# Attention, routing and two MoE layers on one core: the weight-narrowing steps and the first norm moved to other slots of an expert, low parts moved behind the gathers

## The chip, the cores and the metric

One NeuronCore of one Trainium2 chip runs the whole program; the other cores are idle. The metric is the device time of one execution in microseconds (us), as the median of several executions; lower is better. The engines are named as the profile names them: PE is TensorE (matrix products), PEld its weight loads, DVE VectorE, ACT ScalarE, POOL GpSimd, SP SyncE, which here only issues DMAs. A PE product has a granted clock, shown as a share of full speed (1.00 is 2.4 GHz, 0.50 is 1.2 GHz).

## The reference, cut to what matters

```python
for t in range(S):                                  # attention, 4 x 8 heads, 768 steps, head size 48
    state = f[:, :, t, :, None] * state + einsum('bhd,bhe->bhde', k[:, :, t], v[:, :, t])
    y[:, :, t] = einsum('bhd,bhde->bhe', q[:, :, t], state)
x = y, one row of 384 numbers for each of 3072 tokens
logits = x @ w_gate                                 # 8 experts, at most 384 tokens each, highest logits first
for e in range(8):                                  # first layer
    out[tokens of e] = maximum(x[tokens of e] @ w1[e], 0) @ w2[e]      # 384 -> 1024 -> 384
xn = out / sqrt(mean(out * out, axis=-1) + 1e-6) * rms_g               # norm
g = xn @ w_gate2;  val = xn @ w_val                 # second layer, 384 -> 1536
result = (g * sigmoid(g) * val) @ w_out             # 1536 -> 384
```

The three weight matrices of the second layer (`w_gate`, `w_val`, `w_out` of `moe2`) come as 64-bit floats.

## The kernel before, in words

**Stages.** Attention (0 to about 183 us of the span); routing, which finds by bisection which tokens each expert takes (to about 236 us); the eight experts of the first layer, one after the other (to about 464 us); the second layer in eight chunks of 384 tokens (to the end). All instructions of one engine run in the order in which the program issues them, since the schedule is written by hand (`manual_schedule`); between engines only semaphores order the work. PE gets its precision from three products for each fp32 product: an operand is split into a high part (`hi`, rounded to the format that PE multiplies in one pass, float32r) and a low part (`lo`, what is left), and `mm3` (lines 570 to 574) multiplies hi·hi, hi·lo and lo·hi. A high part is a copy on ACT, a low part a subtraction on DVE.

**An expert.** `expert(e)` (lines 1025 to 1045) has eight slots, j = 0 to 7. Slot j multiplies the expert's 384 tokens (`XT[e]`, hi and lo) with 128 columns of w1 (`h`, 9 products at lines 572 to 574), takes the high part with ReLU on ACT (`hh`, line 1036) and the low part on DVE (`hl`, line 1037), and from slot 2 on multiplies what slot j - 2 made with w2 (`second`, tile `x2`, 9 products). The last two `second` follow slot 7. So `hl` of slot j has two slots of PE work before it is due. Then `side(e, j)` (lines 992 to 1023) issues work beside PE:
- slot 0: the gathers of the next expert's token rows (`gather`, line 782, three indirect DMAs on POOL's queue) and a weight load on SP's queue;
- slots 1 to 4: one narrowing step, and one `piece_split` of the next expert's weights: hi by ACT (line 756), lo by DVE (line 759, 1536 numbers in each partition);
- slots 5 to 7: the transposition of one third of the next expert's tokens on PE (`xpose`, line 918, tile `xT`), its hi on ACT (line 928) and its lo on DVE (line 929); in slots 6 and 7 one narrowing step behind it.

**A narrowing step** (`narrow_step`, lines 972 to 978) turns a 36th of the 64-bit weights of the second layer into fp32 in a pipeline over several steps. One call issues, in this order: the write back to memory of a piece finished earlier (a DMA on ACT's queue, line 974), the arithmetic of a piece loaded two calls ago (`narrow2`: line 960 on ACT into `nr`; lines 961, 962 and 964 on DVE, the last into `ne`; lines 965 and 966 on POOL), and the load of another piece (a DMA on SP's queue, line 951). `ne` has one buffer, so line 964 of a step waits until line 965 of the step before has read it; `nb` has two, `nr` and `nraw` three. There are six calls in each of the experts 0 to 6, 42 in all, of which 40 do something.

**The first norm.** `Norm` (lines 853 to 890) of chunk 0 runs in the last expert's slots, by the table `NORM0`: the squares and their sum over the three blocks, with a hi and a lo part of the sum, in slot 0 (`squares`, lines 862 to 872); in slot 1 the sum over partitions, by two float32r products with a matrix of ones, and the square root (`total`, lines 874 to 878); the reciprocals in slots 2 to 4; the three scalings in slot 5; hi and lo of the scaled tokens (`prep`, line 897) in slot 6. The other chunks' norms run in the second layer.

**The seam between routing and expert 0.** `R.finish` ends with the token indices `idx` (line 303). Lines 829 to 832 then issue expert 0's three gathers on POOL, two subtractions for low parts of expert 0's weights on DVE (`low_part(0)` and `low_part(2)`, line 795), and the load of a flag into a register of every engine, on which each of them branches (line 833; the slow path behind it is not taken). Behind it come nine transpositions of the gathered rows (line 1051), the split of the tokens (`split`, lines 926 to 929), and the other two low parts (1 and 3, line 1055). Low part 0 and 1 belong to w1 of expert 0, 2 and 3 to its w2.

Of the kernel before, what the change touches and what calls it, by code (L numbers as in the profile page):

```python
# [7 lines left out]
F32 = mybir.dt.float32  # L8
F32R = mybir.dt.float32r
# [682 lines left out]
def tile_kernel(ctx, tc, q, k, v, f_logit, w_gate, w1, w2, w2_gate, w2_val, w2_out, rms_g, out):  # L692
# [107 lines left out]
    with ExitStack() as st:  # L800
        with tc.tile_pool(name="rw", bufs=6) as rw, tc.tile_pool(name="rwp", bufs=4, space=PSUM) as rwp:
            rows = Rows(tc, YT, x_dram, ident, rw, rwp)
            rows.put(1)
            rows.take(1)
            R = R[0]
            R.copy()
            w_load(0, 0)

            def side(s):
                if s < 0:  # L810
                    bank = rwp.tile([128, 4, 2, 64], F32, name="rows").rearrange("p a b c -> p (a b c)")
                    turn_inc(tc, K, bank[:, 0:128], ident)
                    return
                if s == 0:
                    more_consts(tc, rc, K)
                if s < 3:
                    w_load(0, s + 1)
                if 0 < s < 5:
                    pool, raw, shape, _ = W1[0, s - 1]
                    hi, lo = (pool.tile([128, 1536], F32R, name="w").rearrange("p (a b) -> p a b", a=shape[0])  # L820
                              for _ in range(2))
                    nc.scalar.copy(hi, raw)
                    parts[s - 1] = hi, lo, raw

            R.steps(6, rows, side)
            rows.put(2)
            rows.take(2)
            R.finish(flag, idx, ident, lambda: (rows.put(3), rows.take(3)))
            gather(0)
            for i in (0, 2):  # L830
                low_part(i)
        rv = nc.values_load(flag[0:1, 0:1], min_val=0, max_val=1)
        with tc.If(rv > 0):
            with tc.tile_pool(name="rb", bufs=1, space=PSUM) as rb:
                R.start(NT // 128, rb.tile([128, 256], F32, name="bank"))
            R.copy()
            R.steps(15)
            R.finish(flag, idx, ident)
            rv2 = nc.values_load(flag[0:1, 0:1], min_val=0, max_val=1)
            with tc.If(rv2 > 0):  # L840
                slow_attention(tc, q, k, v, f_logit, x_dram, w_gate, lg, lg_dram, ident)
                slow_route(tc, K, lg, A.rearrange("p e n -> p n e"), ident)
                slots(tc, K, A, ident, idx)
            gather(0)
# [6 lines left out]
    TC = CAP  # L851

    class Norm:


        def __init__(self, c, pool, psum, name, tmp=None, parts=None):
            self.parts = parts or (lambda: [pool.tile([128, TC], F32R, name=n) for n in ("sh", "sl")])
            self.x = xn[:, :, c * TC:(c + 1) * TC]
            self.pool, self.psum, self.name = pool, psum, name
            self.tmp = tmp or (lambda n: pool.tile([128, TC], F32, name=n))  # L860

        def squares(self):
# [4 lines left out]
                nc.scalar.activation(sq, self.x[:, m], AF.Square)  # L867
                nc.vector.tensor_tensor(out=s, in0=s, in1=sq, op=OP.add)
            self.s = s
            self.sh, self.sl = self.parts()  # L870
            nc.scalar.copy(self.sh, s)
            nc.vector.tensor_tensor(out=self.sl, in0=s, in1=self.sh.bitcast(F32), op=OP.subtract)

        def total(self):
            o = self.psum.tile([128, TC], F32, name=self.name)
            nc.tensor.matmul(o, ones, self.sh, start=True, stop=False)
            nc.tensor.matmul(o, ones, self.sl, start=False, stop=True)
            nc.scalar.activation(self.s, o, AF.Sqrt, bias=eps[:, 0:1], scale=1.0 / DM)

        def recip(self, i):  # L880
# [13 lines left out]
    def xt_tiles():  # L894
        return [xtp.tile([128, KD, CAP], F32R, name=n) for n in ("xhi", "xlo")]
# [7 lines left out]
    with ExitStack() as c1:  # L903
# [75 lines left out]

        X0 = []  # L980

        def first_parts():
            X0.extend(xt_tiles())
            return [t[:, 0] for t in X0]

        n0 = Norm(0, tp, psT, "xT", lambda n: nraw().rearrange("p c two -> p (c two)").bitcast(F32)[:, :TC], first_parts)
        NORM0 = {(E - 1, 0): n0.squares, (E - 1, 1): n0.total}
        tail0 = n0.steps()[2:]
        for i in range(2, 5):
            NORM0[E - 1, i] = tail0.pop(0)  # L990

        def side(e, j):
            if e + 1 < E:
                if j == 0:
                    gather(e + 1)
                    w_load(e + 1, 1)
                if 0 < j < 5:
                    narrow_step()
                    piece_split(W1[e + 1, j - 1])
                if j in (1, 2):  # L1000
                    w_load(e + 1, j + 1)
# [2 lines left out]
                if j == 7:  # L1004
                    if e + 2 < E:
                        w_load(e + 2, 0)
                    else:
                        w2_load(0)
                if j > 5:
                    narrow_step()  # L1010
            else:
                if j < 6:
                    w2_load(j + 1)
                if j:
                    piece_split(W2[j - 1])
                if j == 5:
                    for f in tail0:
                        f()
                if j == 6:
                    for d in range(KD):  # L1020
                        prep(0, d, X0, nc.gpsimd)
            if (e, j) in NORM0:
                NORM0[e, j]()

        def expert(e):
# [18 lines left out]
            second(e, KF - 1, x2, H)  # L1044
            finish(e, x2)

        XT[0] = xt_tiles()
        o = x2_tiles()
        for c in range(3):
# [1 line left out]
                nc.tensor.transpose(o[d][:, c * 128:(c + 1) * 128], XG[0][c][:, d * 128:(d + 1) * 128], ident)  # L1051
        for d in range(KD):
            split(0, d, o[d])
        for i in (1, 3):
            low_part(i)
        w_load(1, 0)
        for e in range(E):
# [116 lines left out]
```

## Time and profile before

| | |
|---|---|
| median of 3 executions | 926.68 us |
| lowest, highest | 925.27, 927.19 us |
| the profiled execution | 926.02 us |
| its span, first to last instruction | 924.3 us |
| mean granted clock of PE over the span | 0.968 |
| DVE busy over the span | 502.0 us (54%), 839 instructions |
| ACT busy over the span | 380.7 us (41%), 748 instructions |
| POOL busy over the span | 277.3 us (30%), 328 instructions |

All times of the trace are counted from the span's start. The profiled execution lies inside the spread of the three timed ones; 1.7 us of its time lie outside the span. Shares over the whole span say little about the experts: each stage has to be read by itself.

### The profile page before, as it was taken

The numbers are of one execution on the slowest core, as the hardware profiler recorded it, in microseconds if no ns is written. First come the engines' busy times: TensorE is split into PE (matmuls) and PEld (weight loads), VectorE is DVE, ScalarE is ACT, GpSimd is POOL, SyncE is SP. The second block draws the span as 40 slices with busy tenths as digits, with TensorE's granted clock in tenths as the row PEclk, the third lists the DMA queues.
The fourth block names the chain that finished last, engine by engine and source line by source line (L and its number), as shares of the span: only waits on it lengthen the run. The fifth ranks groups of instructions, "written<-read, shape, count | busy, mean of one in ns | idle before, by whom it ended". The sixth has DMA issues, their size and how long they took to land.

```text
span 924.3 us, 17642 instructions
## 1 busy us (share of the span) xinstructions
PE 876.3 (95%) x7263; PEld 844.5 (91%) x7263; DVE 502.0 (54%) x839; ACT 380.7 (41%) x748; POOL 277.3 (30%) x328
## 2 busy tenths in 40 slices
PE   7999999866699999999999999999999999999997
PEld 7889897755599999999899999999999999999996
DVE  6665666477679888886744333443324333343222
ACT  3444444366245555454752332423324232242221
POOL 3323333154557777773410201102011010100101
PEclk9999999965599999999999999999999999999999
DMA  9556551062567788776320000000000000000000
GB/s 207 122 114 135 110 119 28 1 219 109 190 243 246 248 296 290 266 243 218 104 69 1 26 1 1 27 1 26 1 1 26 1 27 2 1 26 1 26 1 26
DMA packets 70168, 87.73 MB, mean 95 GB/s; under 512 B 29632, under 2 KB 56256, under 8 KB 70080
## 3 DMA queue, kind: packets, MB, share of 16 engines
q1 hardware_dynamic: 61008, 70.00, 26.0%
q0 software_dynamic: 3072, 9.44, 3.1%
q10 hardware_dynamic: 6000, 7.09, 2.2%
q8 instruction: 58, 0.95, 0.4%
q14 instruction: 30, 0.25, 0.1%
HBM read 70.01 MB, written 16.52 MB: 94 GB/s over the span
## 4 chain that ended last, share of the span: by engine, by line
PE 71%; issue 11%; DVE 10%; POOL 3%; DMA 2%; ACT 1%; POOLq 0%; ACTq 0%; SPq 0%; DVEq 0%
PE bank L390 7%; PE yp L484 5%; PE v L574 4%; PE g L573 4%; PE v L573 4%; PE v L572 4%; PE g L574 4%; PE g L572 4%; PE o L573 4%; PE o L572 4%; PE o L574 4%; PE bank L450 3%; PE x L573 2%; PE x L574 2%; PE x L572 2%
## 5 line engine op out<-in xcount | busy, mean ns | idle before, releaser
L1112 DVE TENSOR_TENSOR hf<-sg,v 128x384 f32<-128x384 f32 x96 | 53.1, 553 | 193.8 <-PE v L574 164.6
L900 POOL TENSOR_TENSOR xlo<-xn,xhi 128x384 fp32r<-128x384 f32 x24 | 27.4, 1143 | 302.3 <-ACT xhi L899 302.3
L1115 ACT CAST hh<-hf 128x384 fp32r<-128x384 f32 x96 | 49.3, 513 | 139.0 <-DVE hf L1112 137.3
L573 PE MATMUL o<-w,hh 128*128 128x384 f32 x288 | 97.0, 337 | 0.0
L572 PE MATMUL o<-w,hh 128*128 128x384 f32 x288 | 96.6, 335 | 0.0
L573 PE MATMUL g<-xlo,w 128*128 128x384 f32 x288 | 96.6, 335 | 0.0
L574 PE MATMUL v<-xhi,w 128*128 128x384 f32 x288 | 96.6, 335 | 0.0
L572 PE MATMUL v<-xhi,w 128*128 128x384 f32 x288 | 96.6, 335 | 0.0
L573 PE MATMUL v<-xlo,w 128*128 128x384 f32 x288 | 96.5, 335 | 0.0
L574 PE MATMUL g<-xhi,w 128*128 128x384 f32 x288 | 96.5, 335 | 0.0
L574 PE MATMUL o<-w,hl 128*128 128x384 f32 x288 | 96.3, 334 | 0.0
L572 PE MATMUL g<-xhi,w 128*128 128x384 f32 x288 | 96.2, 334 | 0.0
L1110 ACT ACTIVATE sg<-g 128x384 f32<-128x384 f32 x96 | 47.1, 491 | 118.7 <-PE g L574 118.5
L1116 DVE TENSOR_TENSOR hl<-hf,hh 128x384 fp32r<-128x384 f32 x96 | 53.6, 559 | 55.6 <-ACT hh L1115 55.6
L965 POOL TENSOR_TENSOR nr<-nr,ne 128x384 f32<-128x384 f32 x36 | 62.4, 1734 | 46.5 <-DVE ne L964 17.3
L573 PE MATMUL x<-hl,w 128*128 128x384 f32 x192 | 65.7, 342 | 2.5 <-DVE hl L1037 2.2
L759 DVE TENSOR_TENSOR w<-wraw,w 128x1536 fp32r<-128x1536 f32 x35 | 64.6, 1845 | 5.3 <-ACT w L756 5.2
L572 PE MATMUL h<-xhi,w 128*128 128x384 f32 x192 | 67.1, 349 | 0.3 <-ACT xhi L928 0.3
L573 PE MATMUL h<-xlo,w 128*128 128x384 f32 x192 | 65.7, 342 | 0.0
L574 PE MATMUL h<-xhi,w 128*128 128x384 f32 x192 | 65.5, 341 | 0.0
L572 PE MATMUL x<-hh,w 128*128 128x384 f32 x192 | 65.3, 340 | 0.0
L457 POOL TENSOR_SCALAR_AFFINE_SELECT at<-at 128x384 f32<-128x384 f32 x62 | 31.5, 543 | 111.2 <-ACT at L456 111.1
(231 smaller groups left out, 2034.3 us busy)
## 6 DMA issues: line engine op xcount, KB each, us to landing
wraw<-in_moe_w_dram SPq DMA_DIRECT2D x32, 768.0 KB, 5.9
raw_f<-in_f_logit_dram SPq DMA_DIRECT2D x16, 288.0 KB, 3.4
raw_k<-in_k_dram SPq DMA_DIRECT2D x16, 288.0 KB, 5.0
raw_q<-in_q_dram SPq DMA_DIRECT2D x16, 288.0 KB, 5.0
v<-in_v_dram SPq DMA_DIRECT2D x32, 144.0 KB, 4.6
x_dram<-xrows SPq DMA_DIRECT2D x24, 192.0 KB, 1.9
nraw<-in_moe_w_gate_dram SPq DMA_DIRECT2D x12, 384.0 KB, 5.9
nraw<-in_moe_w_val_dram SPq DMA_DIRECT2D x12, 384.0 KB, 5.2
```

What stands on the lines that cost most here:

```text
L390: nc.tensor.matmul(o[64 * h:64 * h + 64, r * TP:(r + 1) * TP], t[:, c0:c0 + 64], ident[0:TP, 0:TP], start=True, stop=True)
L457: nc.gpsimd.affine_select(out=t, in_=t, pattern=[[0, 3], [1, C]], compare_op=OP.is_ge, fill=0.0, base=0, channel_multiplier=-1)
L484: nc.tensor.matmul(YP[n // 3][d, (n % 3) * C:(n % 3 + 1) * C], ST[i][d, :, n] if state else V[i % NV][:, n, h, :], QT[i][d, c] if state el ...
L572: nc.tensor.matmul(out, lhs[0], rhs[0], start=first, stop=False)
L573: nc.tensor.matmul(out, lhs[0], rhs[1], start=False, stop=False)
L574: nc.tensor.matmul(out, lhs[1], rhs[0], start=False, stop=last)
L759: eng.tensor_tensor(out=lo, in0=raw, in1=hi.bitcast(F32), op=OP.subtract)
L965: nc.gpsimd.tensor_tensor(out=r, in0=r, in1=e2.bitcast(F32), op=OP.mult)
L1110: nc.scalar.activation(sg, pg, AF.Silu)
L1112: nc.vector.tensor_tensor(out=h, in0=sg, in1=pv, op=OP.mult)
L1115: nc.scalar.copy(hh, h)
L1116: nc.vector.tensor_tensor(out=hl, in0=h, in1=hh.bitcast(F32), op=OP.subtract)
```

## The change

Three edits, all in what the hand-written order issues where.

1. The six narrowing steps of an expert stand in slots 0, 1, 4, 5, 6 and 7 instead of 1, 2, 3, 4, 6 and 7. In slot 0 the step stands behind the gathers and the weight load; in slots 5 to 7 behind the transposition.
2. The first norm's squares move from slot 0 of expert 7 to slot 7 of expert 6, behind everything else there, and its total from slot 1 to slot 0 of expert 7. For this chunk alone the sum isn't split: one fp32 product with ones takes the place of two float32r products, and a copy on ACT and a subtraction on DVE fall away. The reciprocals move to slots 1 to 3; scaling and `prep` of block 0, 1 and 2 stand in slots 4, 5 and 6, where `X0` is also allocated now.
3. `low_part(0)` moves behind the branch, ahead of expert 0's transpositions; `low_part(2)` moves behind the split, ahead of low parts 1 and 3.

```diff
@@ -827,8 +827,6 @@
             gather(0)
-            for i in (0, 2):
-                low_part(i)
         rv = nc.values_load(flag[0:1, 0:1], min_val=0, max_val=1)
...
@@ -867,14 +865,19 @@
             self.s = s
-            self.sh, self.sl = self.parts()
+            if not self.parts:
+                return
+            self.sh, self.sl = (self.pool.tile([128, TC], F32R, name=n) for n in ("sh", "sl"))
             nc.scalar.copy(self.sh, s)
...
         def total(self):
             o = self.psum.tile([128, TC], F32, name=self.name)
-            nc.tensor.matmul(o, ones, self.sh, start=True, stop=False)
-            nc.tensor.matmul(o, ones, self.sl, start=False, stop=True)
+            if self.parts:
+                nc.tensor.matmul(o, ones, self.sh, start=True, stop=False)
+                nc.tensor.matmul(o, ones, self.sl, start=False, stop=True)
+            else:
+                nc.tensor.matmul(o, onesf, self.s, start=True, stop=True)
...
-        NORM0 = {(E - 1, 0): n0.squares, (E - 1, 1): n0.total}
+        NORM0 = {(E - 2, 7): n0.squares, (E - 1, 0): n0.total}
         tail0 = n0.steps()[2:]
-        for i in range(2, 5):
+        for i in range(1, 4):
             NORM0[E - 1, i] = tail0.pop(0)
...
                     gather(e + 1)
                     w_load(e + 1, 1)
+                if j in (0, 1, 4):
+                    narrow_step()
                 if 0 < j < 5:
-                    narrow_step()
                     piece_split(W1[e + 1, j - 1])
...
-                if j > 5:
+                if j > 4:
                     narrow_step()
...
-                if j == 5:
-                    for f in tail0:
-                        f()
-                if j == 6:
-                    for d in range(KD):
-                        prep(0, d, X0, nc.gpsimd)
+                if j == 4:
+                    X0.extend(xt_tiles())
+                if 3 < j < 7:
+                    tail0[j - 4]()
+                    prep(0, j - 4, X0, nc.gpsimd)
...
+        low_part(0)
         XT[0] = xt_tiles()
...
         for d in range(KD):
             split(0, d, o[d])
-        for i in (1, 3):
+        for i in (2, 1, 3):
             low_part(i)
```

## Rows read from the trace of the kernel before

**Rows 1.** The page, section 1: busy us, share of the span, instructions

```profile
PE 876.3 (95%) x7263; PEld 844.5 (91%) x7263; DVE 502.0 (54%) x839; ACT 380.7 (41%) x748; POOL 277.3 (30%) x328
```

**Rows 2.** Waits of PE over the span: total us, times, longest us

```profile
PE x L1051 <- DMA xrow<-x_dram,idx: 6.7, 2, 6.0
...
PE x L573 <- DVE hl L1037: 2.2, 3, 0.8
```

**Rows 3.** Timeline of all engines at the seam: start us, us, what, [idle before]

```profile
236.38 3.43 DVE L795 TENSOR_TENSOR w<-wraw,w 128x1536 fp32r<-128x1536 f32 x2
236.47 2.75 POOL L782 DMA_INDIRECT xrow<-x_dram,idx  x1 [1.45 <-DVE idx L303]
239.52 1.11 POOL L782 DMA_INDIRECT xrow<-x_dram,idx  x1 [0.30 <-issue]
240.94 0.94 POOL L782 DMA_INDIRECT xrow<-x_dram,idx  x1 [0.30 <-remote]
...
245.23 0.69 PE L572 MATMUL h<-xhi,w 128*128 128x384 f32 x1 [0.28 <-ACT xhi L928]
...
246.61 3.42 DVE L795 TENSOR_TENSOR w<-wraw,w 128x1536 fp32r<-128x1536 f32 x2
...
249.95 0.55 DVE L1037 SCALAR_TENSOR_TENSOR hl<-h,hh 128x384 fp32r<-128x384 f32 x1
...
252.49 0.34 PE L573 MATMUL x<-hl,w 128*128 128x384 f32 x1
```

**Rows 4.** Line 833 (the branch) on DVE: ns min/median/max, first and last start

```profile
L833 DVEq EVENT_SEMAPHORE  x2: 21/21/21, 240.5 to 240.6; - x2
...
L833 DVEq COMPARE_BRANCH  x1: 72/72/72, 237.1 to 237.1; - x1
```

**Rows 5.** Table by stretch, all engines; PEclk is the granted clock

```profile
248.00:252.00 4.00, 4.00 (x20) 4.00 (x19) 3.03 (x4) 1.55 (x3) 0.00 (x0) 0.76 0.93 308
```

**Rows 6.** The same table: experts 1 to 6 together, expert 3, expert 4

```profile
273.79:436.63 162.84, 160.38 (x919) 157.02 (x919) 137.19 (x186) 87.26 (x141) 115.27 (x84) 1.00 0.79 264
328.00:355.62 27.62, 26.88 (x155) 26.20 (x154) 24.26 (x34) 14.87 (x25) 20.90 (x15) 1.00 0.80 265
355.62:382.37 26.75, 26.66 (x154) 26.23 (x154) 23.27 (x34) 14.78 (x25) 20.07 (x15) 1.00 0.81 269
```

**Rows 7.** Timeline of DVE in expert 3, slots 1 to 4

```profile
332.38 0.35 DVE L961 TENSOR_SCALAR nb<-nraw 128x384 int32<-128x384 int32 x1
...
333.77 1.76 DVE L759 TENSOR_TENSOR w<-wraw,w 128x1536 fp32r<-128x1536 f32 x1
...
340.96 0.55 DVE L1037 SCALAR_TENSOR_TENSOR hl<-h,hh 128x384 fp32r<-128x384 f32 x1
341.43 0.70 DVE L961 TENSOR_SCALAR nb<-nraw 128x384 int32<-128x384 int32 x1
...
343.80 1.75 DVE L759 TENSOR_TENSOR w<-wraw,w 128x1536 fp32r<-128x1536 f32 x1
```

**Rows 8.** Timeline of POOL in expert 3, slots 0 and 1

```profile
331.22 0.99 POOL L782 DMA_INDIRECT xrow<-x_dram,idx  x1
...
333.85 2.50 POOL L782 DMA_INDIRECT xrow<-x_dram,idx  x1 [0.30 <-issue]
336.37 1.03 POOL L965 TENSOR_TENSOR nr<-nr,ne 128x384 f32<-128x384 f32 x1
```

**Rows 9.** Timeline of PE at the first norm in expert 7

```profile
441.59 0.44 PE L876 MATMUL xT<-xhi,onesr 128*128 128x384 f32 x1 [1.61 <-ACT xhi L871]
442.18 0.44 PE L877 MATMUL xT<-xlo,onesr 128*128 128x384 f32 x1 [0.15 <-DVE xlo L872]
442.46 0.34 PE L572 MATMUL h<-xhi,w 128*128 128x384 f32 x1
442.64 0.34 PE L573 MATMUL h<-xlo,w 128*128 128x384 f32 x1
```

**Rows 10.** Groups of instructions, shapes apart: count, busy us, mean ns of one

```profile
L496 PE MATMUL bank<-YT,wgp 112*32 112x384 f32 x64 | 6.4, 492 | 0.0
```

More of the change, by code (lines that the diff above doesn't have):

```diff
@@ L853, in tile_kernel, with __init__ @@
     class Norm:
-        def __init__(self, c, pool, psum, name, tmp=None, parts=None):
-            self.parts = parts or (lambda: [pool.tile([128, TC], F32R, name=n) for n in ("sh", "sl")])
+        def __init__(self, c, pool, psum, name, tmp=None, parts=True):
+            self.parts = parts
             self.x = xn[:, :, c * TC:(c + 1) * TC]
@@ L980, in tile_kernel @@
         X0 = []
[L982 to L986, printed above, removed]
-        NORM0 = {(E - 1, 0): n0.squares, (E - 1, 1): n0.total}
+        n0 = Norm(0, tp, psT, "xT", lambda n: nraw().rearrange("p c two -> p (c two)").bitcast(F32)[:, :TC], False)
+        NORM0 = {(E - 2, 7): n0.squares, (E - 1, 0): n0.total}
         tail0 = n0.steps()[2:]
-        for i in range(2, 5):
+        for i in range(1, 4):
             NORM0[E - 1, i] = tail0.pop(0)
```

## The prediction, made before the changed kernel ran

> **What bounds the kernel now.** The page first: PE is busy for 95% of the span [rows 1], so time is to be had only where PE stands still or its clock is low. The table of waits of PE gives the places: 6.7 us at the transpositions of expert 0's gathered rows, and 2.2 us for `hl`, the low part of the hidden block, in the experts [rows 2]. The first norm adds 1.61 and 0.15 us [rows 9]. The table of waits understates: a product is shown as 0.34 us long although the next starts 0.18 us behind it (442.46 to 442.64) [rows 9], so the first 0.16 us of every wait hides in its length. Hence the table by stretch: experts 1 to 6 take 162.84 us, 27.14 each, with expert 4 at 26.75 and expert 3 at 27.62 [rows 6]. An expert needs 144 products a little under 0.18 us apart, about 25.6, and nine transpositions, which I put at 0.8 together, less than the 1.1 that expert 4 leaves: 26.4. What is above that is waiting for DVE, whose queue holds 23.3 to 24.3 us of work in each [rows 6].
>
> **Part one, the seam.** In the timeline the first gather takes 2.75 us on POOL, the next two 1.11 and 0.94. Two low parts start on DVE 0.09 us ahead of it and take 3.43 together, so the first ends at 238.10; the gather ends at 239.22, just a plain gather (1.12) later [rows 3]. Expert 3 shows it again: a gather issued 0.08 us behind a weights' low part takes 2.50, one without such company 0.99 [rows 7, 8]. I read it as the gather waiting for the subtraction. The Trainium skill, "SBUF — State Buffer", section "Who interferes with whom", says that a tensor_tensor with two SBUF inputs holds up only GpSimd work that reads SBUF, and that descriptor generation needs the write side, so a gather would not be stopped; both rows speak against that. By that rule this part would bring nothing; it is a rival below.
>
> Without the low parts the three gathers take 1.1, 1.11 and 0.94 with two gaps of 0.30, and end at 240.22 instead of 241.88: 1.66 us earlier. From there to the first `h` product it is 3.35 us (to 245.23) [rows 3], landing and transpositions, unchanged. Does low part 0 get in the way again? DVE branches at 237.1 and its first instruction behind the branch stands at 240.5 [rows 4]; these 3.4 us put low part 0 at about 240.5 to 242.2, behind the third gather and ahead of the split. Behind the split DVE now has three low parts where it had two (3.42, so 1.71 each): they start at 246.61 - 1.66 = 244.95, end at 250.08, and `hl` of slot 0 is ready by 250.6, with the product that needs it due at 252.49 - 1.66 = 250.83 [rows 3]. So that cover is 0.2 us, and gone if PE gets any faster; what is late next is this `hl`, which caps the gain at 1.9. The clock: the stretch 248 to 252 has a mean of 0.76 [rows 5], so it rises from 0.50 to 1.00 at about 249.9. If the rise comes earlier with the work, 1.66 is kept; if it stays where it is, the work done in the time gained runs at half speed and is worth 0.83. Bounds 0.8 and 1.9; I take **1.4**, nearer to the work moving as a whole.
>
> **Part two, the narrowing steps.** A step costs DVE 1.39 us alone (332.38 to 333.77), and 2.37 beside POOL's products (341.43 to 343.80), since lines 961 and 962 then wait for POOL; an `hl` or token low part costs 0.47 (340.96 to 341.43), a weights' low part 1.75 [rows 7]. Before, slots 1 to 4 hold hl, step and low part: 0.47 + 2.37 + 1.75, less overlaps, is 4.5 us a slot (340.96 to 345.55, where the low part of 343.80 ends) where PE needs 18 products, 3.2. DVE falls behind by 1.3 a slot, and slots 6 and 7 wait for `hl`. After, slots 2 and 3 hold 2.2 each and DVE catches up; slots 4 to 7 and the idle start of the expert take the steps.
>
> But a step issues more than DVE work. In slot 0 its POOL products queue behind three gathers, the first of which starts 3.2 us into the expert (331.22 against 328.00) [rows 6, 8]; with 1.3 for each they end at about 7.0, and line 965 (1.03) [rows 8] at 8.0. The step of slot 1 follows at once, and its `ne` has to wait for that line 965. DVE gets there at 2.2 (first `h`, 1.6, and its high part, some 0.5) + 0.47 + 1.7 + 0.47 + 1.1 = 5.9: **a new wait of 2 us**, with slot 1's weights' low part and `hl` of slot 2 queued behind it. Then the queue runs: `ne` 8.3; low part of slot 1, held 0.7 by POOL, 10.7; hl 11.1 (due 11.2); low part, held 0.4, 13.2; hl 13.7; low part, held 0.4, 15.8; hl 16.2; step 17.6; low part 19.3; hl and token part 20.2; step beside POOL 22.4; hl and token part 23.3; step 25.2 (its first lines meet less of POOL); hl of slot 7 at 25.7. It is due one product into the last nine of 26.4, at 25.0: 0.7 late. So experts 2 to 5 take 27.1; the high part behind that `hl` and lags between engines add 0.1. Expert 1 starts with an empty queue and expert 6 has arithmetic in two steps only: 26.5 each. 4 x 27.2 + 53.0 = 161.8 against 162.84: **1.0** less. The other queues: SP's weight load stays ahead of the narrowing load in slot 0, and both have two slots until used; ACT's write back in slot 0 must land before line 960 of slot 1 may write `nr`, behind which the high part of slot 2 waits, due only at 11. Bounds: all waiting gone, 158.4 (-4.4); a third gather or a late write back in every expert, +3.
>
> **Part three, the norm.** PE stands 1.61 + 0.16 us ahead of the first product with ones, and from there to the next `h` it is 0.87 where two products need 0.36: 2.28 in all [rows 9]. After, the sum is ready in time: from the end of slot 0's `h` (436.63 + 1.6) [rows 6] to the product at 441.59 the chain of squares, sums and split took 3.4; from the transposition in expert 6's slot 7 to the total in expert 7's slot 0 PE has 27 products, 4.8. The fp32 product: no such one is in the trace. The nearest is the logits' product, also fp32 with 384 columns, 32 of the array's columns wide, 0.49 us in a burst of 64 that keep PE busy for 6.4 [rows 10]; bounds are 0.18 (a product of two rounded operands) and 0.49, and I take 0.36, which is what two cost. Gain **2.2**. ACT's copy and DVE's subtraction that fall away lay beside this wait. The scalings and `prep` spread over slots 4 to 6 and end no later than before; PE didn't wait for them.
>
> **Sum.** 1.4 + 1.0 + 2.2 = 4.6 us: 926.02 becomes 921.4 for an execution like the profiled one. That one lay 0.66 under the median of 926.68, so I forecast a median of **922.1**. About 0.2%, 1.9 us, is what a measurement of this kernel can tell from no change.
>
> **Rivals.**
> - *DVE catches up fully* and experts 1 to 6 run at 26.4: 4.4 instead of 1.0, 918.7. For it: DVE's own work, 24 us, fits [rows 6]. Against: the new wait for `ne`. 0.14.
> - *The seam doesn't move*: the first gather is slow for being the first, or low part 0 comes through the branch early and lands on the second: 0 instead of 1.4, 923.5. Against: the rows of expert 3. 0.10. The page's rule named above would give this time.
> - *The experts gain nothing*: late write backs or POOL's order eat 1 to 3 us more than summed, 923 to 925.4. 0.20.
> - *Slower*: the wait for `ne` grows. If in slot 0 or 1 one gather meets a two-input DVE instruction of the step beside it and takes 2.50 instead of 0.99 [rows 8], line 965 and all of DVE's queue come 1.5 later in each of experts 1 to 5: 7.5 more, 929.6. For it: it happened in expert 3, not in 4. Against: the long low part now stands behind `ne`, so only line 962 is near. From 0.55 us an expert the gain is no longer to be told from nothing, from 1.3 the kernel is slower. 0.06.
>
> **Numbers.** The forecast, 921 to 924, has 0.50. Faster by over 0.2% means under 924.8: forecast, full catch-up, unmoved seam and some half of the third rival, 0.83; slower only the last, 0.06; the rest 0.11. The range runs from 918.5 to 925.4.
>
> **What would show it.** The first gather near 1.1 us, the first `h` near 243.6, low part 0 behind 240; DVE idle ahead of line 964 in slot 1 for about 2 us, experts 2 to 5 near 27.2, with the waiting in the last product block instead of slots 6 and 7; no wait at the total of the norm, and expert 7 2.2 shorter. A first gather still at 2.7, or experts over 27.6, would prove the steps wrong.

## The result, and the profile after

The changed kernel takes 932.78 us (median of 4 executions, 932.41 to 933.08), the kernel before, beside it, 926.43 (925.27 to 927.19). The ratio is 1.0069, with a 95% interval of 1.0052 to 1.0087: slower by 6.3 us, where the forecast was 922.1 and the range ended at 925.4. The profiled execution took 932.51, with a span of 930.8 against 924.3 before. The page, section 1, in the columns of [rows 1]:

```profile
PE 879.9 (95%) x7263; PEld 847.1 (91%) x7263; DVE 499.2 (54%) x838; ACT 381.2 (41%) x747; POOL 264.5 (28%) x328
```

PE does the same 7263 products, and DVE and POOL are busy for less time than before; so the 6.5 us are again waiting, and a low clock behind it: PE is busy for 3.6 us more. The table by stretch says where. Its rows after: expert 0; experts 1 to 5 together; expert 3; expert 6; expert 7 (columns as in [rows 6], the granted clock third from the end).

```profile
243.58:272.64 29.06, 29.06 (x153) 28.65 (x154) 25.42 (x33) 14.15 (x23) 11.17 (x12) 0.90 0.73 248
272.64:409.39 136.75, 133.41 (x766) 130.05 (x766) 115.76 (x165) 75.32 (x121) 98.27 (x75) 1.00 0.77 265
326.99:354.44 27.45, 26.80 (x155) 26.09 (x155) 23.36 (x34) 14.95 (x25) 19.61 (x16) 1.00 0.78 266
409.39:439.59 30.20, 28.17 (x154) 27.73 (x154) 17.99 (x25) 14.26 (x24) 9.34 (x10) 0.94 0.68 238
439.59:470.80 31.21, 28.05 (x148) 26.55 (x147) 20.52 (x19) 17.98 (x24) 10.07 (x5) 0.95 0.23 77
```

Cut at the start of each expert's first product, the difference of the two spans splits as follows:

| stretch | before | after | difference |
|---|---|---|---|
| start to `idx` | 236.10 | 235.74 | -0.36 |
| `idx` to the first `h` | 9.13 | 7.84 | -1.29 |
| expert 0 | 28.56 | 29.06 | +0.50 |
| experts 1 to 5 | 136.19 | 136.75 | +0.56 |
| expert 6 | 26.65 | 30.20 | +3.55 |
| expert 7 | 27.84 | 31.21 | +3.37 |
| second layer | 459.84 | 459.99 | +0.15 |

The first row, what runs ahead of the change, moves by itself: `idx` stands between 235.09 and 237.61 in the profiles of this case. Two experts carry the loss, and in both the mean clock is under 1.00; before it was 1.00 in experts 1 to 6 [rows 6] and in expert 7:

```profile
436.63:464.47 27.84, 26.07 (x147) 25.49 (x147) 20.64 (x22) 19.59 (x28) 12.33 (x5) 1.00 0.26 86
```

The waits of PE (columns as in [rows 2]) name the engines:

```profile
PE x L573 <- DVE hl L1036: 5.4, 8, 2.0
PE x L1051 <- remote: 5.1, 1, 5.1
...
PE x L572 <- ACT hh L1035: 2.9, 2, 2.3
```

The wait at the transpositions fell from 6.7 to 5.7 (5.1, and 0.6 for the gathers' landing), `hl` rose from 2.2 to 5.4, and a wait for `hh` is new: 2.9 us in two pieces. Line 1035 after is line 1036 before; `narrow2` moved by three lines (964 became 967, 965 became 968).

**The seam.** Timeline of all engines, as in [rows 3]:

```profile
236.12 1.21 POOL L782 DMA_INDIRECT xrow<-x_dram,idx  x1 [1.44 <-DVE idx L303]
...
238.90 0.95 POOL L782 DMA_INDIRECT xrow<-x_dram,idx  x1 [0.30 <-issue]
240.08 1.76 DVE L795 TENSOR_TENSOR w<-wraw,w 128x1536 fp32r<-128x1536 f32 x1 [4.18 <-DVEq L831]
...
243.58 0.69 PE L572 MATMUL h<-xhi,w 128*128 128x384 f32 x1 [0.28 <-ACT xhi L931]
...
244.96 5.09 DVE L795 TENSOR_TENSOR w<-wraw,w 128x1536 fp32r<-128x1536 f32 x3
```

The first gather takes 1.21 instead of 2.75, the low part stands behind all three, and the first `h` comes 1.29 earlier behind `idx`. The inference of the Trainium skill ("SBUF — State Buffer", "Who interferes with whom"), by which a two-input DVE instruction leaves descriptor generation alone, does not hold for these gathers: 2.75 with the low parts in front, 1.21 without. They also read their indices; whether that read or the writing of descriptors is what waits isn't shown.

**An ordinary expert**, expert 3, slots 0 to 2, timeline of all engines, as in [rows 7, 8]:

```profile
332.37 0.56 DVE L965 SCALAR_TENSOR_TENSOR nb<-nraw,nb 128x384 int32<-128x384 int32 x1
...
333.01 0.95 POOL L782 DMA_INDIRECT xrow<-x_dram,idx  x1 [0.30 <-issue]
...
333.98 1.03 POOL L968 TENSOR_TENSOR nr<-nr,ne 128x384 f32<-128x384 f32 x1
...
335.05 0.36 DVE L967 TENSOR_SCALAR ne<-nb 128x384 int32<-128x384 int32 x1 [2.12 <-POOL nr L968]
...
335.32 2.57 DVE L759 TENSOR_TENSOR w<-wraw,w 128x1536 fp32r<-128x1536 f32 x1
```

The third gather takes 0.95 where it took 2.50, and in its place DVE stands 2.12 us for `ne`; the low part behind it then meets POOL's next products and takes 2.57 where 1.76 is its length alone.

**The norm.** Timeline of PE, as in [rows 9]:

```profile
441.18 0.81 PE L880 MATMUL xT<-nraw,onesf 128*128 128x384 f32 x2
441.53 0.63 PE L572 MATMUL h<-xhi,w 128*128 128x384 f32 x1
442.00 0.33 PE L573 MATMUL h<-xlo,w 128*128 128x384 f32 x1
```

No wait is left. The fp32 product shows as two records, and from its start to the second `h` behind it 0.82 pass; with one `h` of 0.17 in it the product costs 0.65.

**Where expert 6 loses.** Timeline of all engines, slots 0 to 2 (SPq and ACTq are the DMA issues of SP and ACT):

```profile
407.34 1.60 SPq L749 DMA_DIRECT2D wraw<-in_moe_w_dram  x3
...
411.24 0.33 ACTq L977 DMA_DIRECT2D w_o<-nr  x1
...
417.96 0.56 ACT L963 ACTIVATE nr<-nraw 128x384 f32<-128x384 uint32 x1 [4.70 <-DMA w_o<-nr]
...
418.42 1.47 ACT L756 CAST w<-wraw 128x1536 fp32r<-128x1536 f32 x1
...
419.80 0.47 ACT L1035 ACTIVATE hh<-h 128x384 fp32r<-128x384 f32 x1
...
419.92 2.45 DVE L759 TENSOR_TENSOR w<-wraw,w 128x1536 fp32r<-128x1536 f32 x1 [2.12 <-ACT w L756]
...
422.29 0.55 DVE L1036 SCALAR_TENSOR_TENSOR hl<-h,hh 128x384 fp32r<-128x384 f32 x1
...
422.89 0.44 PE L573 MATMUL x<-hl,w 128*128 128x384 f32 x1 [2.03 <-DVE hl L1036]
```

Three weight loads stand in SP's queue together, since the last narrowing load is out, and the write back issued at 411.24 lands only at about 417.9 (the median of such a write back to `w_o` is 3.2 us from issue to landing). That the loads delay it is a guess from the order of issue and was not tried apart. ACT waits 4.70 us for it, in front of the high part of the weights and of `hh`; DVE's low part and `hl` come behind them, and PE stands 2.03. Before, the loads and ACT's wait were there as well, but the wait stood one slot later, with the `hh` of slot 2 (415.62) already ahead of it, and PE stood next to nowhere in that expert (timeline of ACT, kernel before):

```profile
415.62 0.47 ACT L1036 ACTIVATE hh<-h 128x384 fp32r<-128x384 f32 x1
419.79 0.56 ACT L960 ACTIVATE nr<-nraw 128x384 f32<-128x384 uint32 x1 [3.69 <-DMA w_o<-nr]
```

**Where expert 7 loses.** Timeline of all engines, slots 4 to 6 of the changed kernel:

```profile
453.33 3.51 POOL L759 TENSOR_TENSOR w<-wraw,w 128x1536 fp32r<-128x1536 f32 x1 [2.45 <-ACT w L756]
453.69 3.56 DVE L889 SCALAR_TENSOR_TENSOR xn<-xn,gcol,nraw 128x384 f32<-128x384 f32 x1
...
459.59 1.76 DVE L759 TENSOR_TENSOR w<-wraw,w 128x1536 fp32r<-128x1536 f32 x1 [0.80 <-ACT w L756]
...
461.26 0.61 DVE L889 SCALAR_TENSOR_TENSOR xn<-xn,gcol,nraw 128x384 f32<-128x384 f32 x1
...
461.91 0.51 ACT L902 CAST xhi<-xn 128x384 fp32r<-128x384 f32 x1 [2.35 <-DVE xn L889]
...
462.32 0.48 ACT L1035 ACTIVATE hh<-h 128x384 fp32r<-128x384 f32 x1
...
462.71 1.47 ACT L756 CAST w<-wraw 128x1536 fp32r<-128x1536 f32 x1
...
464.21 1.76 DVE L759 TENSOR_TENSOR w<-wraw,w 128x1536 fp32r<-128x1536 f32 x1 [0.81 <-ACT w L756]
...
465.88 0.61 DVE L889 SCALAR_TENSOR_TENSOR xn<-xn,gcol,nraw 128x384 f32<-128x384 f32 x1
466.53 0.51 ACT L902 CAST xhi<-xn 128x384 fp32r<-128x384 f32 x1 [2.35 <-DVE xn L889]
466.94 0.48 ACT L1035 ACTIVATE hh<-h 128x384 fp32r<-128x384 f32 x1
...
467.48 0.52 PE L572 MATMUL x<-hh,w 128*128 128x384 f32 x1 [2.35 <-ACT hh L1035]
```

This is a ring. The copy of `prep` (902) waits on ACT for the scaling of the same slot (889); the scaling stands behind DVE's low part (759); that waits for ACT's high part (756), which stands behind the `hh` that stands behind the copy of the slot before. One turn is 4.62 us (461.91 to 466.53), where PE needs 18 products, 3.2. PE falls back to ACT's pace and stands 0.60 and then 2.35. The ring is entered late: the first scaling takes 3.56 us beside a low part of 3.51 on POOL, where the next two take 0.61. Behind both long waits, 2.03 in expert 6 and 2.35 here, the clock is low (table by stretch, 4 us each):

```profile
424.00:428.00 4.00, 4.00 (x17) 4.00 (x17) 4.00 (x5) 1.40 (x2) 0.00 (x0) 0.66 0.94 341
468.00:472.00 4.00, 3.93 (x16) 3.93 (x15) 1.78 (x2) 2.23 (x4) 0.12 (x1) 0.61 0.00 0
```

### The profile page after: what moved, and what is told of

The parts are those of the page before. It is cut to its first block, busy times and chain, and to the rows that moved or that the text cites. A ratio compares the mean times of both kernels' runs of the same rounds, so it can differ in the third digit from the quotient of the medians.

```text
span 930.8 us, 17625 instructions
## 1 busy us (share of the span) xinstructions
PE 879.9 (95%) x7263; PEld 847.1 (91%) x7263; DVE 499.2 (54%) x838; ACT 381.2 (41%) x747; POOL 264.5 (28%) x328
## 4 chain that ended last, share of the span: by engine, by line
PE 47%; issue 11%; DVE 8%; POOL 3%; DMA 3%; ACT 2%; POOLq 0%; SPq 0%; DVEq 0%; ACTq 0%
PE v L574 4%; PE v L572 4%; PE v L573 4%; PE g L574 4%; PE g L573 4%; PE g L572 4%; PE o L573 4%; PE o L572 4%; PE o L574 4%; DVE w L759 2%; DVE nb L965 2%; DVE hl L1036 2%; DMA wraw<-in_moe_w_dram 2%; PE x L573 2%; PE x L574 1%
## 5 line engine op out<-in xcount | busy, mean ns | idle before, releaser
L903 POOL TENSOR_TENSOR xlo<-xn,xhi 128x384 fp32r<-128x384 f32 x24 | 24.4, 1015 | 310.9 <-ACT xhi L902 310.9
L759 DVE TENSOR_TENSOR w<-wraw,w 128x1536 fp32r<-128x1536 f32 x35 | 70.1, 2002 | 9.9 <-ACT w L756 9.7
L572 PE MATMUL x<-hh,w 128*128 128x384 f32 x192 | 66.3, 345 | 2.9 <-ACT hh L1035 2.9
L968 POOL TENSOR_TENSOR nr<-nr,ne 128x384 f32<-128x384 f32 x36 | 52.5, 1458 | 50.4 <-ACT nr L963 20.8
L574 PE MATMUL x<-hh,w 128*128 128x384 f32 x192 | 65.7, 342 | 0.0
```

The costliest lines, as they stand in the source:

```text
L572: nc.tensor.matmul(out, lhs[0], rhs[0], start=first, stop=False)
L574: nc.tensor.matmul(out, lhs[1], rhs[0], start=False, stop=last)
L759: eng.tensor_tensor(out=lo, in0=raw, in1=hi.bitcast(F32), op=OP.subtract)
L903: eng.tensor_tensor(out=X[1][:, d], in0=s, in1=X[0][:, d].bitcast(F32), op=OP.subtract)
L968: nc.gpsimd.tensor_tensor(out=r, in0=r, in1=e2.bitcast(F32), op=OP.mult)
```

## The experiments

Theory after the result: A, the ring at the end of expert 7 costs 5.6 us; B, the late write back costs expert 6 of the changed kernel some 3.5 us; C, the rest of the narrowing edit and the seam gain next to nothing. Lengths of stretches below come from one profiled execution of each kernel, the medians from all its executions.

### Each edit by itself

**seam_alone**, the kernel before with the third edit only:

```diff
             gather(0)
-            for i in (0, 2):
-                low_part(i)
...
+        low_part(0)
         XT[0] = xt_tiles()
...
-        for i in (1, 3):
+        for i in (2, 1, 3):
             low_part(i)
```

> The kernel before with edit 3 alone (low parts 0 and 2 moved). Theory: the first gather waited for low part 0; the first h product comes 1.3 to 1.7 us earlier after the indices, as in the changed kernel, nothing gives it back later: 925.2, between 924.6 and 925.8. Rival: the three low parts behind the split eat it, and the time is that of before, 926.4.

Measured: 926.8 against 926.1, ratio 1.0002 (0.9992 to 1.0012): no change. From `idx` to the first `h` it is 7.52, 1.61 less than before, as summed, and expert 0 takes 28.41 instead of 28.56, so the three low parts behind the split, the rival's reason, eat nothing. But the gain is given back. The profiled execution was the longest of the ten (928.08); 1.5 of that is `idx`, which came at 237.61, ahead of the edit. In it the third gathers of experts 2 to 6 all take 2.5; in the kernel before expert 4 had one of 0.94, and expert 4 now takes 27.60 instead of 26.75. And the wait at the first norm's total, the same 1.61 us as in [rows 9], is followed by a low clock, which it was not before (timeline of PE; then the table by stretch, expert 7):

```profile
442.07 0.45 PE L874 MATMUL xT<-xhi,onesr 128*128 128x384 f32 x1 [1.61 <-ACT xhi L869]
```

```profile
437.11:466.50 29.39, 27.63 (x147) 27.05 (x147) 19.60 (x22) 19.70 (x28) 12.35 (x5) 0.94 0.25 81
```

Expert 7 takes 29.39 instead of 27.84: 1.55 for a clock that drops or not behind the same wait.

**narrow_alone**, the kernel before with the first edit only:

```diff
+                if j in (0, 1, 4):
+                    narrow_step()
                 if 0 < j < 5:
-                    narrow_step()
                     piece_split(W1[e + 1, j - 1])
...
-                if j > 5:
+                if j > 4:
                     narrow_step()
```

> The kernel before with edit 1 alone (narrowing steps in slots 0, 1, 4 to 7). Theory: experts 1 to 5 come out even (27.46 each against a mean of 27.24 before), expert 6 loses 3.5 us, because line 960 of slot 1 waits for the write back that slot 0 issued and the high part of slot 2 stands behind it on ACT: 930.5, expert 6 at 30 us with one stretch at clock 0.50. Rival: the loss in expert 6 comes from the norm's squares, which now stand in its slot 7: then expert 6 stays under 27 here and the time is 926 to 927.5.

Measured: 929.77, ratio 1.0046 (1.0030 to 1.0063), 3.7 us slower by itself. Experts 1 to 6 take 165.7 where they took 162.84 [rows 6]; expert 6 27.58, with the same wait of ACT (4.32), a wait of PE of 0.97 behind it and, in the profiled execution, no low clock. So B doesn't need the other edits, but here it costs 0.9, not 3.5. That the time came near the 930.5 expected is in part luck: the larger loss in this profile is expert 4 (28.58 instead of 26.75, with a wait of PE of 1.28 for `hl` at its end), which the theory had at no loss.

**norm_alone**, the kernel before with the second edit only:

```diff
-        NORM0 = {(E - 1, 0): n0.squares, (E - 1, 1): n0.total}
+        NORM0 = {(E - 2, 7): n0.squares, (E - 1, 0): n0.total}
...
-                if j == 5:
-                    for f in tail0:
-                        f()
-                if j == 6:
-                    for d in range(KD):
-                        prep(0, d, X0, nc.gpsimd)
+                if 3 < j < 7:
+                    tail0[j - 4]()
+                    prep(0, j - 4, X0, nc.gpsimd)
```

> The kernel before with edit 2 alone (first norm earlier, one fp32 product, scaling and prep spread over slots 4 to 6). Theory: 2.0 us gained at the total, 5.5 lost at the end of expert 7, where scaling, copy, high part and weights' low part of three slots wait for one another between DVE and ACT: 929.9. Rival: the 5.5 us come from weights of the second layer that land late since the narrowing steps write them later: then nothing is lost here, and the time is 924.4.

Measured: 930.07, ratio 1.0046 (1.0029 to 1.0063). Expert 7 takes 31.20 as in the changed kernel, and the others are as before. The loss of expert 7 is the norm edit's alone.

### Undoing the two losses

**tail_back**, the changed kernel with scalings and `prep` where they were:

```diff
-                if 3 < j < 7:
-                    tail0[j - 4]()
-                    prep(0, j - 4, X0, nc.gpsimd)
+                if j == 5:
+                    for f in tail0:
+                        f()
+                if j == 6:
+                    for d in range(KD):
+                        prep(0, d, X0, nc.gpsimd)
```

> The changed kernel with the three scalings back in slot 5 and all of prep back in slot 6 of expert 7; squares, total and reciprocals stay early. Theory: the 5.5 us ahead of the second layer are gone, with the stretch at clock 0.50 there: 927.3, and from the last reciprocal to the first g product no wait of PE over 0.3. Rival: late weights of the second layer, then the wait stays and the time is 932.8.

Measured: 925.05, ratio 0.9992 (0.9981 to 1.0003): 7.7 us under the changed kernel. Table by stretch, expert 6 and expert 7:

```profile
410.76:438.28 27.52, 26.57 (x154) 26.14 (x154) 17.56 (x25) 14.26 (x24) 10.73 (x10) 1.00 0.75 261
438.28:463.90 25.62, 25.62 (x147) 25.35 (x147) 18.28 (x19) 17.83 (x24) 12.29 (x5) 1.00 0.28 93
```

Expert 7 falls from 31.21 to 25.62, 5.6, which shows A. Expert 6 takes 2.7 less, and so the time is under the 927.3 expected: ACT's wait is 4.30 instead of 4.70 and the weights' low part behind it 1.76 instead of 2.45, so PE stands 0.95 instead of 2.03 and the clock stays up. Experts 3 and 4 take 0.5 and 0.6 more. One execution of the ten took 929.18; whether the clock fell in its expert 6 isn't known.

**tail_stagger**, the other proof of the ring: everything stays in its slot, but `prep` of a block stands one slot behind its scaling, so that ACT's copy finds it done.

```diff
-                if 3 < j < 7:
-                    tail0[j - 4]()
-                    prep(0, j - 4, X0, nc.gpsimd)
+                if j > 4:
+                    prep(0, j - 5, X0, nc.gpsimd)
+                if 3 < j < 7:
+                    tail0[j - 4]()
```

> The changed kernel with prep of each block one slot behind its scaling (slots 5 to 7 instead of 4 to 6), scalings left in slots 4 to 6. Theory: what costs is that ACT's copy of a block waits for the scaling of the same slot, and the next slot's high part stands behind that copy; a slot apart neither waits: expert 7 at 25.6 to 26 instead of 31.2, time 925 to 926. Rival: the scalings themselves, the first held 3 us by POOL's low part, make DVE late: expert 7 stays above 29 and the time above 928.5.

Measured: 926.77, ratio 1.0009 (0.9998 to 1.0019). Expert 7 (table by stretch):

```profile
438.36:464.89 26.53, 25.90 (x147) 25.31 (x147) 21.39 (x19) 17.93 (x24) 13.21 (x5) 1.00 0.28 90
```

Of the 5.6 us 4.7 are gone, though the first scaling still takes 3.56 beside POOL: the copy behind a scaling of its own slot is what costs. The spreading keeps 0.9, more than expected, with PE waiting 0.63 for an `hl` near the end. What the ring would cost without that first long scaling was not tried.

**back_other_buffer**, tail_back with the last piece's `nr` in a free `nraw` buffer, so that the step in slot 1 of expert 6 waits for no write back:

```diff
-            r = tp.tile([128, n], F32, name="nr", bufs=3)
+            r = nraw().rearrange("p c two -> p (c two)").bitcast(F32)[:, :n] if last else tp.tile([128, n], F32, name="nr", bufs=3)
```

> As tail_back, but the last piece's nr lies in a free nraw buffer, so that line 963 (960 before) in slot 1 of expert 6 has no write back to wait for. Theory: ACT's wait of 4.3 us there is gone, expert 6 falls from 27.5 (30.2 where the clock drops) to 26.8 or less, and the time from 925.05 to 924.2, with no execution near 929. Rival: ne behind the gathers and the low part held by POOL make expert 6 late; then it stays at 27.5 and some executions at 929.

Measured: 924.39, ratio 0.9978 (0.9968 to 0.9988). Timeline of ACT, then the table by stretch for expert 6:

```profile
416.61 0.56 ACT L963 ACTIVATE nraw<-nraw 128x384 f32<-128x384 uint32 x1
```

```profile
412.73:439.30 26.57, 26.57 (x154) 26.16 (x154) 18.59 (x25) 14.49 (x24) 12.24 (x10) 1.00 0.76 269
```

ACT writes without waiting, PE is busy throughout, and expert 6 is down to 26.57, what it took before (26.65). That shows that the wait for the write back is what expert 6 loses by, and prices it at 0.95 where the clock stays up. The 3.5 of the changed kernel, with a stand of PE twice as long and a low clock behind it, is read from its trace and wasn't taken apart. The medians, 925.05 and 924.39 with intervals that overlap, don't show 0.95; in this profile, the longest of the nine, experts 1 and 2 take 28.05 and 28.80 instead of 26.87 and 27.47, which nothing here explains.

### What is left in the experts

**back_gather_late**, tail_back with the gathers in slot 2 instead of slot 0, to take the wait for `ne` away:

```diff
                 if j == 0:
-                    gather(e + 1)
                     w_load(e + 1, 1)
+                if j == 2:
+                    gather(e + 1)
```

> As tail_back, with the gathers of the next expert moved from slot 0 to slot 2, behind the weights' split, so that POOL has slot 0's products before them. Theory: DVE's wait of 2 us for line 968 ahead of ne in slot 1 is gone and experts 1 to 5 fall from 27.5 towards 26.7: 921 to 922.5. Rival: DVE's queue is full anyway and the last hl stays late, because the low parts and POOL's products hold each other; then experts stay at 27.2 or more and the time is 924 to 925.

Measured: 960.94, ratio 1.0377 (1.0345 to 1.0409), a miss that says nothing on `ne`: the rows now come too late for the transpositions in slots 5 to 7, and the clock falls after these waits too. Waits of PE:

```profile
PE xT L926 <- DMA xrow<-x_dram,idx: 25.7, 15, 3.0
```

**step_first**, back_other_buffer with the step of slot 0 ahead of the gathers, so that POOL's products come first:

```diff
                 if j == 0:
-                    gather(e + 1)
                     w_load(e + 1, 1)
                 if j in (0, 1, 4):
                     narrow_step()
+                if j == 0:
+                    gather(e + 1)
```

> As back_other_buffer, with slot 0's narrowing step issued ahead of the three gathers on POOL instead of behind them. Theory: the wait of 2 us for line 968 ahead of ne in slot 1 goes, since that product no longer queues behind the gathers, and the gathers, 2 us later, still land 5 us before slot 5's transposition: experts 2 to 5 fall from 27.5 to 26.6 to 26.8, the time from 924.4 to 921.0 to 921.8. Rival: the later gathers meet slot 1's low part and slot 1's products stand behind them, so the waiting only moves: experts at 27.2 or more, time 924 to 925.

Measured: 927.03, ratio 1.0000 (0.9985 to 1.0014). The wait for `ne` is gone (line 967 shows none). Timeline of all engines, expert 3:

```profile
338.14 0.36 DVE L967 TENSOR_SCALAR ne<-nb 128x384 int32<-128x384 int32 x1
...
341.28 1.83 POOL L782 DMA_INDIRECT xrow<-x_dram,idx  x1 [0.31 <-issue]
```

Experts 3 and 4 fall to 26.95, 0.5 under the changed kernel's; experts 1 and 6 take 27.80 and 28.06. The gathers are later and again beside low parts (1.83 here), and expert 0 rises to 31.65, with waits of PE for `hl`: there the gathers of expert 1 start at 248.34 only (243.05 in the changed kernel), behind fills of the load buffers that wait for DVE. The time is 927, not the 921 expected, and over the rival's 925 too. **step_first_after**, the same edit on the changed kernel, says the same at its level:

> The changed kernel with that one edit: slot 0's narrowing step ahead of the gathers. Theory: experts 1 to 5 gain 3 to 4 us together as in step_first; in expert 6 the late write back still holds ACT, so 0 to 1 there; the end of expert 7 stays at 31.2: 928 to 930. Rival: 932 to 933, as the changed kernel.

Measured: 934.6, ratio 1.0090 (1.0075 to 1.0104), with experts 2 and 3 at 27.0, expert 0 at 31.72 and expert 7 at 31.13.

### The parts that gain

**seam_norm**, the kernel before with the seam edit and the norm's early squares, early total and single fp32 product, but the scalings, `prep` and the narrowing steps where they were (against the changed kernel, tail_back's diff and this):

```diff
-                if j in (0, 1, 4):
-                    narrow_step()
                 if 0 < j < 5:
+                    narrow_step()
                     piece_split(W1[e + 1, j - 1])
...
-                if j > 4:
+                if j > 5:
                     narrow_step()
```

> The kernel before with edit 3 and the early norm with one fp32 product, but scaling and prep as before and the narrowing steps where they were. Theory: 1.5 us at the seam less 0.5 for the clock, 2.2 at the norm, nothing lost: 922.9, between 922 and 924.5 as the third gather falls ahead of or behind a weights' low part. Rival: what the seam gains is given back in the experts, as its own run at 926.8 could say: then only 2.2 remain, 924.

Measured: 923.52, ratio 0.9971 (0.9960 to 0.9981): faster than both kernels. Nearly all of it is the norm's: expert 7 takes 25.63 instead of 27.84. Of the seam's 1.2 from `idx` to the first `h` little is kept, since expert 0 takes 0.5 more and experts 1 to 6 163.9 instead of 162.84 [rows 6]. Beside back_other_buffer, timed with it, it is 0.9 less, with intervals that overlap: with both losses mended, the moved steps bring nothing that shows.

**split_later** was to take the last suspect away. It is seam_norm with the splits of the next expert's weights one slot later, so that no low part meets the third gather; **split_later_before** is the same edit on the kernel before.

```diff
                 if 0 < j < 5:
                     narrow_step()
-                    piece_split(W1[e + 1, j - 1])
+                if 1 < j < 6:
+                    piece_split(W1[e + 1, j - 2])
```

> The seam and norm edits with the old narrowing slots, and the four splits of an expert's weights one slot later (slots 2 to 5 instead of 1 to 4), so that no low part stands beside the third gather. Theory (in these experts it is the third gather, held by the low part of slot 1, that keeps experts 2 to 5 at 27.6 and 28.0 instead of 26.75): all gathers take 0.9 to 1.1, experts 2 to 5 take 26.7 to 26.9 each, 3.8 less together, and the median falls from 923.5 to about 919.7. Rival (the experts are bound by the sum of DVE's work, wherever it stands): the low part that is now in slot 5 makes hl of slots 6 and 7 as late as before, experts 2 to 5 stay at 27.4 or more, and the median stays at 923 to 924.

> The kernel before with nothing but the four splits one slot later. Theory (third gather): experts 2, 3 and 5 go from 27.6 to 26.75 as expert 4 had it, 2.6 less, so about 923.9 against 926.5; experts 6 and 7 unchanged. Rival (the sum of DVE's work): no change, 926.5.

Measured: 924.93, ratio 0.9988 (0.9979 to 0.9997), and 929.69, ratio 1.0037 (1.0023 to 1.0051). The theory falls; both times are over their rivals' as well (923 to 924, and 926.5). Timeline of all engines, split_later, expert 3:

```profile
333.88 0.95 POOL L782 DMA_INDIRECT xrow<-x_dram,idx  x1 [0.30 <-issue]
...
335.90 0.36 DVE L967 TENSOR_SCALAR ne<-nb 128x384 int32<-128x384 int32 x1 [1.35 <-POOL nr L968]
...
336.18 2.57 DVE L759 TENSOR_TENSOR w<-wraw,w 128x1536 fp32r<-128x1536 f32 x1
```

The third gather takes 0.95, and expert 3 still 27.56: DVE now stands 1.35 for `ne` instead, and its low part meets POOL's products again. On the kernel before, expert 4 even rises from 26.75 to 28.34, and expert 7 to 29.32. Free one of gather, `ne` and low part, and the next takes its place. In experts 1 to 5 of the kernel before and of seam_alone the third gather and the expert's length go together (about 2.5 us with 27.5 to 27.6, 0.94 to 1.06 with 26.6 to 26.75), so expert 4 came through before because its gather did; but split_later shows that a short gather alone doesn't bring 26.75. Which of DVE's waits binds, and what let the gather of expert 4 alone pass, stays open.

## Why the prediction was wrong

**The norm, the step that failed.** "The scalings and `prep` spread over slots 4 to 6 and end no later than before; PE didn't wait for them": priced at nothing, it cost 5.6 us (31.21 against 25.62 in tail_back). The sentence looked at when the work ends, and not at what queues behind it: ACT's copy is a new wait for DVE, and `hh` and the next high part stand behind it. Asking who waits for ACT would have closed the ring on paper, since each of its members has a row in the trace of the kernel before. The gain of 2.2 was right in sum (27.84 to 25.62 and 25.63), in part by luck. One term was not right: the fp32 product costs 0.65, not 0.36 and over the upper bound of 0.49, so some 0.2 of the gain must have come from elsewhere in the expert, which I didn't trace. The 0.49 was no bound on a cost: 64 such products keep PE busy for 6.4 us [rows 10], 0.1 each, so it is the length of one of several under way, of 32 columns only.

**The narrowing steps, the other one.** "ACT's write back in slot 0 must land before line 960 of slot 1 may write `nr`, behind which the high part of slot 2 waits, due only at 11" named the right wait and took ordinary experts for all of them. In expert 6 that wait ends 8.6 us into the expert (417.96 against 409.39). What then counts is not the high part of slot 2 alone but the chain of it: the weights' high part 1.47 between `nr` and `hh`, DVE's low part of 2.45, then `hl`, at 12.9. PE wanted that `hl` at 420.7, 11.3 into the expert. The cost in this one expert, 3.5 (0.9 in tail_back and narrow_alone, where the clock stayed up), is above the bound of "+3" that was given for all of them; its arithmetic in two steps only was taken for a relief ("26.5 each").

In experts 1 to 5 the mechanism was right almost to the number. DVE was to reach `ne` at 5.9 and to be done with it at 8.3; in expert 3 it got there at 5.9 and was done at 8.42 (335.05 and 0.36, against 326.99). The `hl` behind it was to be ready at 11.1 and was at 11.4; the `hl` of slot 7 was to be ready at 25.7 and was at 25.9. PE's one wait stands there, in the last product block as forecast, and is 0.64 to 0.66 in experts 2 to 5, where 0.7 was summed. Experts 2 to 5 were to take 27.2 and took 27.4 to 27.5; expert 1 was to take 26.5 and took 26.9. What was mis-sized is the base of 26.4: expert 6 takes 26.65 in the kernel before and 26.57 in back_other_buffer with PE busy throughout, some 0.2 more. So a gain of 0.9 in these five (135.3 summed, 136.19 before) became a loss of 0.56 even before expert 6: experts 2, 3 and 5, which had waited some 0.75 before, gain 0.13 to 0.17 each; expert 4, which had next to no wait, loses 0.74, and expert 1 loses 0.27.

**The seam.** Right at its place in mechanism, wrong in what is kept. Counted from `idx`, which came 0.36 earlier in this execution, the gathers end at 4.11 (4.12 summed) and low part 0 starts at 4.34 (4.4 summed). But from the gathers' end to the first `h` it is 3.73 where 3.35 was put as unchanged (3.42 in seam_alone), so the gain is 1.29 and not 1.66, and the three low parts start at 9.22 (8.85 summed). That the first `h` still stands at 243.58 in the trace, where 243.6 was named, is luck. Then the granted clock came out near the lower bound: the stretch 248 to 252 has a mean of 0.84 (0.76 in [rows 5]), which puts the rise at about 249.3 instead of 249.9, and expert 0 is 0.5 longer (0.15 shorter in seam_alone). From `idx` to the first product of expert 1 the gain is 0.8, the lower end given, not 1.4. That the rest goes in later experts (seam_alone shows no net gain) had no term at all. In the profiles of seam_alone and seam_norm the largest part of it in experts 1 to 6 is expert 4, whose third gather now takes 2.50 like the others' (27.60 instead of 26.75); why an earlier start brings that about stays open.

**The rivals.** The slower one had a chance of 0.06 and a mechanism that did not happen: after the seam all gathers of the changed kernel but one take 0.9 to 1.3 us (the third of those issued in expert 0 takes 1.98). "The experts gain nothing" named late write backs, with a price of 1 to 3 us more than summed and an end at 925.4 (922.1 and 3 make 925.1); that was the right place for half the loss. No rival had PE standing long enough for the clock to fall, and that made the losses larger: with PE's stand 1.1 shorter and the clock up, expert 6 took 27.52 in tail_back, against 30.20 here.

## What to carry to other kernels

When a step is moved, write down for every engine it issues on what is queued right behind it and who waits for that, also for steps that "end no later": a copy that waits for a result of its own slot stops everything behind it (5.6 us here), and one that stands a slot later cost 0.9. Look at the last round of a pipeline by itself, since where one kind of load has run out, the others may bunch. An engine whose short waits follow one another may give little back when one of them is removed, and a wait of PE of some two microseconds should be priced with a low clock behind it.

## What the runs showed of the hardware

- The clock fell behind waits of PE of 2.03 and 2.35 us, and behind one of 1.61 in seam_alone where the same 1.61 in the kernel before cost nothing more. The price was about 1.5 us (expert 7 at 29.39 against 27.84). What decides between the two isn't shown by these runs.
- One fp32 product with ones shows as two records and costs 0.65 us, nearly as much as four of the 0.17 us that a product of rounded operands takes.
- A write back of 192 KB issued after three weight loads of 768 KB took some 6.7 us (411.24 to 417.96), twice the 3.2 of the median; in the kernel before, at the same place, 6.4 (413.42 to 419.79), against a median of 4.2. That the loads are the reason isn't shown.
- Some work of DVE and of POOL gets longer where it overlaps: a scaling of 0.61 us takes 3.56 beside a subtraction of 3.51 on POOL, a low part of 1.76 takes 2.57 beside POOL's products, and a gather of 0.95 to 1.2 takes 2.50 or 2.75 behind a low part.
